# Chunked attention and a multiplicative FFN on one core: the first q and k as float32 through SyncE's queue, DMA transposes from group 12, another order of the first loads

## The chip, the cores and the metric

The kernel runs on one core of a Trainium2 chip. The core has five engines with queues of their own: TensorE (PE, matrix products and transposes), VectorE (DVE), ScalarE (ACT), GpSimd (POOL) and SyncE (SP). POOL and SP are used here to issue DMAs. The DMAs of both run on the same 16 DMA engines. The metric is the device time of one execution in microseconds (us). A time is the median of several runs; a profile is one execution, recorded by the hardware profiler.

## The reference

Eight batches of eight heads, 576 tokens and 64 columns per head go through softmax attention in chunks of 64 tokens; a chunk sees only itself. The heads are then put side by side (4608 tokens x 512 columns) and go through four weight matrices with one elementwise product:

```python
scores = scale * np.matmul(q_c, k_c.transpose(0, 1, 2, 4, 3))     # chunks of 64
scores = scores - np.max(scores, axis=-1, keepdims=True)
attn = np.exp(scores)
attn = attn / (np.sum(attn, axis=-1, keepdims=True) + 1e-09)
out = np.matmul(attn, v_c)
...
x = out.transpose(0, 2, 1, 3).reshape(B * S, H * D)               # 4608 x 512
a = x @ w1                                                        # 512 -> 1024
b = x @ w2
h = a * b @ w3                                                    # 1024 -> 1024
return (h @ w_out).astype(np.float32)                             # 1024 -> 512
```

All inputs and the output are float32 in DRAM.

## The kernel before

The kernel computes in bfloat16. Since no nonlinearity stands between w3 and w_out, it first multiplies the two once (w3o = w3 @ w_out, eight blocks of 128 rows, add_w3o) and then runs the FFN as (a * b) @ w3o.

The attention is cut into 36 groups of two chunks (128 tokens), all eight heads at once (add_group). For a group q and k are loaded (load_qk, line 220, two DMAs of 128 KB in bfloat16 through POOL's queue, which changes the type on the way; four half ones where a group crosses two batches, as group 4 does) into one of six "raw" buffers, tokens in the partitions. The products need the columns in the partitions, so q and k are transposed in one of two ways:

- on PE: eight transposes of 128 x 128 against an identity matrix (t_emit, line 274) into the one PSUM buffer p_tr, and then three copies by DVE or ACT: k to kT, and the two halves of q to a block-diagonal buffer qd (k_copy, q_copy);
- by DMA: one transposing DMA that SP issues (qk_turn, line 281) into kqT, from which k is used as it stands and q is copied to qd.

TURN_QK (line 23) says which group goes which way: 0 to 15 on PE, 16 to 35 by DMA. Then come the scores (s_emit, line 301, eight small matmuls into p_sc), maximum, difference, exponential, sum and normalisation on DVE and ACT, the transpose of the weights "an" (again on PE, at_emit with a copy, or by DMA, at_turn; TURN_A, line 24: by DMA from group 26), the product with v (av_emit, line 345) and the copy to xt.

The FFN goes over nine tiles of four groups (512 tokens, add_tile): for each of eight column blocks four matmuls with w1 and four with w2 (line 432), a copy and a product, and then four blocks of eight matmuls with w3o (line 457), a copy and an output write that SP issues.

No loop sets the order of all this. Every piece of work is an operation with a cost, a key and what it must wait for, and a planner (Plan.run, line 74) simulates the five engines ahead of time: each free engine takes the ready operation with the smallest key. POOL is the exception: it takes its operations, which are the loads and the making of the identity, in the order in which they are added, and that is the list LOADS (line 17), then the rest of the groups. A DMA occupies its engine's queue for its "issue", then moves along a ring; the planner lets two rings that are busy at once share the time in halves, and data count as landed after a further lag. At most eight DMAs are out on a ring. The order that comes out of the simulation is the order of each engine's program; on the chip an engine then keeps that order, and waits in it.

The PSUM is full: four "ffn" buffers, which the w3 blocks and the FFN share, and one each for p_sc, p_at, p_av and p_tr. At the beginning DVE clears the three qd and three vd buffers (lines 206 to 209).

Of the kernel before, what the change touches and what calls it, by code (L numbers as in the profile page):

```python
# [13 lines left out]

LOADS = [("wo", 0, 4), ("w3", 0, 1), ("ident",), ("qk", 0), ("qk", 1), ("wo", 4, 8), ("w3", 1, 2), ("qk", 2),
         ("w3", 2, 3), ("w3", 3, 4), ("qk", 3), ("w3", 4, 5), ("w3", 5, 6), ("qk", 4), ("qk", 5), ("w3", 6, 7),
         ("w12", 0, 2), ("v", 0), ("w3", 7, 8), ("qk", 6), ("qk", 7), ("w12", 2, 4), ("qk", 8), ("w12", 4, 6),
         ("v", 1), ("w12", 6, 8), ("qk", 9), ("qk", 10)]  # L20
TILES = [4] * 9

TURN_QK = [g >= 16 for g in range(36)]
TURN_A = [g >= 26 for g in range(36)]


class Op:
# [12 lines left out]
class Plan:  # L40
# [33 lines left out]
    def run(self):  # L74
        free = {e: 0.0 for e in ("PE", "ACT", "DVE", "POOL", "SP")}
        free["POOL"] = free["SP"] = 1.2
        todo = {e: [o for o in self.ops if e in o.engines] for e in free}

        rings, flown = {"POOL": [], "SP": []}, 0.0
        left, now, order, ends = len(self.ops), 0.0, [], [1.2]  # L80

        def heads(t):
            return [r[0] for r in rings.values() if r and r[0][0] <= t]

        while left or any(rings.values()):

            while flown < now:
                h = heads(flown)
                step = min([now - flown] + [x[1] * len(h) for x in h])
                step = min([step] + [r[0][0] - flown for r in rings.values() if r and r[0][0] > flown])  # L90
                flown = now if step >= now - flown else flown + step
                for x in h:
                    x[1] -= step / len(h)
                for r in rings.values():
                    if r and r[0] in h and r[0][1] < 1e-6:
                        o = r.pop(0)[2]
                        o.end = flown + o.lag
                        ends.append(o.end)
            for eng in free:
                if free[eng] > now or len(rings.get(eng, ())) >= self.RING:  # L100
                    continue
                if eng == "POOL":
                    pick = [o for o in todo[eng][:1] if self.ready(o, now)]
                else:
                    pick = [o for o in todo[eng] if self.ready(o, now)]
                if not pick:
                    continue
                o = min(pick, key=lambda o: o.key)
                for e in o.engines:
                    todo[e].remove(o)  # L110
                o.start, o.engine = now, eng
                cost = o.cost[o.engines.index(eng)] if isinstance(o.cost, tuple) else o.cost
                if o.issue:
                    free[eng] = now + o.issue
                    rings[eng].append([free[eng], cost, o])
                else:
                    free[eng] = now + cost
                    o.end = now + cost + o.lag
                    ends.append(o.end)
                for n in o.takes:  # L120
                    self.taken[n].append(o)
                order.append(o)
                ends.append(free[eng])
                left -= 1
            ends = [t for t in ends if t > now]
            h = heads(now)
            after = ends + [flown + x[1] * len(h) for x in h]
            assert after or not left, "the plan is stuck"
            now = max(min(after, default=now), now + 1e-6)
        return order  # L130
# [3 lines left out]
def kernel(  # L134
# [21 lines left out]
    C = 64  # L156
# [12 lines left out]
    bf = mybir.dt.bfloat16  # L169
    f32 = mybir.dt.float32  # L170

    BUFS = {"raw": 6, "kqT": 4, "kT": 3, "qd": 3, "vd": 3, "sd": 2, "e": 2, "an": 4, "at": 6, "w3t": 2, "abT": 2,
            "a_sb": 3, "o_sb": 4, "ffn": 4, "p_sc": 1, "p_at": 1, "p_av": 1, "p_tr": 1}

    consts = ctx.enter_context(tc.tile_pool(name="consts", bufs=1))
# [4 lines left out]
    def sb(tag, shape, dt=bf, bufs=None):  # L180
        return work.tile(shape, dt, tag=tag, name=tag, bufs=bufs or BUFS[tag])

    def ps(tag, shape, dt=f32):
        return psum.tile(shape, dt, tag=tag, name=tag, bufs=BUFS[tag])

    ident = consts.tile([P, P], bf)
    w1_sb = wpool.tile([P, KO, D_FF], bf, tag="w1")
    w2_sb = wpool.tile([P, KO, D_FF], bf, tag="w2")
    w3_sb = wpool.tile([P, FO, D_FF], bf, tag="w3")
# [22 lines left out]
    def load(cost, issue, emit, **kw):  # L212
        return plan.add("POOL", cost, 0, emit, lag=landing, issue=issue, **kw)
# [6 lines left out]
    def load_qk(g):  # L220
        (b0, c0), (b1, c1) = chunks(g)
        parts = [(slice(0, P), b0, c0, 2)] if b0 == b1 else [(halves[0], b0, c0, 1), (halves[1], b1, c1, 1)]
        box = raws[g] = {"ops": []}
        for w, src in enumerate((q, k)):
            for r, b, c, n in parts:
                def emit(eng, w=w, src=src, r=r, b=b, c=c, n=n):
                    if "t" not in box:
                        box["t"] = sb("raw", [P, 2, H, D])
                    nc.gpsimd.dma_start(box["t"][r, w], src[b, :, c * C:(c + n) * C, :].rearrange("h p d -> p h d"))  # L229
                box["ops"].append(load(0.43 * n, 0.5 + 0.2 * n, emit, takes=() if box["ops"] else ("raw",)))  # L230

    def load_v(b):
        v_got[b] = []
        for t in range(2):
            def emit(eng, t=t):
                nc.gpsimd.dma_start(vds[b % len(vds)][halves[t], :, :, t * D:(t + 1) * D].rearrange("p m c d -> p (m c) d"),  # L236
                                    v[b, NM * t:NM * (t + 1)].rearrange("h (c p) d -> p (h c) d", p=C))
            v_got[b].append(load(2.2, 1.17, emit, takes=() if t else ("vd",), after=(zero_v[b % len(vds)],)))

    def load_w12(j0, j1):  # L240
        for dst, w in ((w1_sb, moe_w1), (w2_sb, moe_w2)):
# [25 lines left out]
    def add_group(g, kt, ks, ka, kv):  # L267
# [6 lines left out]
        def t_emit(eng):  # L274
            t = box["tr"] = ps("p_tr", [P, 2, NM, P], bf)
            raw = raws[g]["t"]
            for w in (1, 0):
                for s in range(NM):
                    nc.tensor.transpose(t[:, w, s, :], raw[:, w, 2 * s:2 * s + 2, :].rearrange("p h d -> p (h d)"), ident[:])  # L279

        def qk_turn(eng):
            t = sb("kqT", [P, 2 * NM, P])
            nc.sync.dma_start_transpose(t[:], raws[g]["t"].rearrange("p w h d -> p (w h d)"))
            box["tr"] = t.rearrange("p (w s) t -> p w s t", w=2)
            box["kT"] = box["tr"][:, 1]
# [4 lines left out]

        def k_copy(eng):
            box["kT"] = sb("kT", [P, NM, P])
            copy(eng, box["kT"][:], box["tr"][:, 1, :, :])

        def q_copy(u):
            def emit(eng):
                copy(eng, qd[halves[u], :, :, u * C:(u + 1) * C].rearrange("p cc s t -> p s cc t"),
                     box["tr"][halves[u], 0, :, :].rearrange("p s (cc t) -> p s cc t", cc=2))
            return emit

        def s_emit(eng):
# [53 lines left out]

        got = raws[g]["ops"]
        if turned:
            tr = kc = plan.add("SP", 2.0, kt, qk_turn, after=got, takes=("kqT",), uses=[(got[0], "raw")], lag=2.5, issue=1.3)
            held, cost = [(tr, "kqT")], (0.35, 0.6)
        else:  # L360
            tr = plan.add("PE", 0.46, kt, t_emit, after=got + [made_ident], takes=("p_tr",), uses=[(got[0], "raw")], lag=0.2)
            held, cost = [(tr, "p_tr")], (0.43, 0.66)
            kc = plan.add(("DVE", "ACT"), cost, kt, k_copy, after=(tr,), takes=("kT",), uses=held)
# [7 lines left out]
        sm = plan.add("DVE", 1.1, ks, sum_emit, after=(ex,), lag=0.05)  # L371
        an = plan.add("DVE", 0.7, ks, norm_emit, after=(sm,), takes=("an",), uses=[(ex, "e")])
        if TURN_A[g]:
            ac = plan.add("SP", 1.0, ka, at_turn, after=(an,), takes=("at",), uses=[(an, "an")], lag=2.5, issue=1.3)
        else:
            at = plan.add("PE", 0.23, ka, at_emit, after=(an,), takes=("p_at",), uses=[(an, "an")], lag=0.2)
            ac = plan.add(("DVE", "ACT"), (0.43, 0.66), ka, at_copy, after=(at,), takes=("at",), uses=[(at, "p_at")])
# [99 lines left out]
    for what, *args in LOADS:  # L477
        if what == "ident":
            made_ident = plan.add("POOL", 0.6, 0, lambda eng: make_identity(nc, ident[:]), lag=0.3)
        else:  # L480
            {"qk": load_qk, "v": load_v, "w12": load_w12, "w3": load_w3, "wo": load_wo}[what](*args)
    landing = 2.5
# [5 lines left out]
            load_v(b)  # L488

    for g in range(NG):  # L490
        late = min(5 if g < 26 else 3, g // 2)
        add_group(g, *(3 * g - n + late for n in (30 if TURN_QK[g] else 28, 25, 19, 16)))
    for ko in range(FO):
        add_w3o(ko, 0.5 + ko)
# [2 lines left out]
        add_tile(g0, n, lambda j: 3 * g0 + 0.375 * n * j, lambda tk: 3 * (g0 + n) + 1 + 3 * tk)  # L497
        g0 += n
    for c, emit in sorted(outs, key=lambda x: x[0].key):
        plan.add("SP", 0.8, c.key, emit, after=(c,), uses=[(c, "o_sb")], lag=1.6, issue=0.4)  # L500

    with tc.manual_schedule():
        for o in plan.run():
# [31 lines left out]
```

## Time and profile before

| | |
|---|---|
| median of 3 runs | 257.01 us (256.85 to 257.58) |
| the profiled execution | 257.51 us, its span 255.7 us |
| PE busy (matmuls; weight loads) | 238.2 us, 93%; 125.9 us, 49% |
| DVE, ACT, POOL busy | 177.5 us (69%), 153.6 us (60%), 102.2 us (40%) |
| granted TensorE clock | 1.0 of full speed |
| DMA queue of POOL (software) | 118,688 packets, 19.41 MB |
| DMA queue of SP (hardware) | 31,888 packets, 16.00 MB |

The span is the time from the first to the last instruction that the profiler shows; the 1.8 us between it and the execution's time lie around it. "Busy" is the sum of an engine's instructions, and matmuls overlap, so a busy PE says little of how well it is used. The page's picture of the span in 40 slices of 6.4 us shows, for each, the busy tenths (9 is 90% or more) and the rate of the DMA engines:

```profile
PE   0469989899999999999999999999999999999994
...
DVE  7569999876989778788887877777768772222310
...
POOL 8856887989790964723392272000000000000000
...
GB/s 81 163 195 178 180 163 175 162 164 155 169 175 149 205 152 179 186 195 181 183 181 199 182 143 149 185 175 108 105 92 73 62 65 62 41 74 52 41 82 123
```

PE reaches nine tenths in the fourth slice. The DMA engines move 150 to 200 GB/s (bytes as written, so bfloat16 for the loads) from the second slice to the 27th, where the loads are through.

The DMAs by kind, with the median time from issue to landing:

```profile
raw<-in_q_dram POOLq DMA_DIRECT2D x32, 128.0 KB, 6.9
raw<-in_k_dram POOLq DMA_DIRECT2D x32, 128.0 KB, 6.7
...
kqT<-raw SPq DMA_TRANSPOSE x20, 7.0
...
at<-an SPq DMA_TRANSPOSE x10, 2.5
```

### The profile page before, as it was taken

Reading aid. Unit: us, or ns where it says so; the run is one execution under the profiler, and the core shown is the slowest. Engines: PE = TensorE matmul, PEld = TensorE weight load, DVE = VectorE, ACT = ScalarE, POOL = GpSimd, SP = SyncE. Lnnn points to the kernel's source line nnn. Section 1 sums busy time; section 2 is a strip of 40 time slices with the busy share of each in tenths; the row PEclk is TensorE's granted clock in tenths of the full one; section 3 lists DMA queues with packets and bytes.
Section 4 is the critical chain, followed back from the end, with each engine's and each line's share of the span. In section 5 each row is a group of like instructions: output and inputs, shape, how many; then the busy total and the mean of one; then the engine's idle time right before and its main releaser. Section 6 shows DMA issues by size and latency. Waiting matters only on the chain.

```text
span 255.7 us, 4814 instructions
## 1 busy us (share of the span) xinstructions
PE 238.2 (93%) x1808; PEld 125.9 (49%) x1808; DVE 177.5 (69%) x338; ACT 153.6 (60%) x268; POOL 102.2 (40%) x128
## 2 busy tenths in 40 slices
PE   0469989899999999999999999999999999999994
PEld 0345655456555555555555555444555444444443
DVE  7569999876989778788887877777768772222310
ACT  2247758668988776676766677756675443433232
POOL 8856887989790964723392272000000000000000
PEclk9999999999999999999999999999999999999999
DMA  5999999999999999999999999985422222111123
GB/s 81 163 195 178 180 163 175 162 164 155 169 175 149 205 152 179 186 195 181 183 181 199 182 143 149 185 175 108 105 92 73 62 65 62 41 74 52 41 82 123
DMA packets 150598, 35.70 MB, mean 140 GB/s; under 512 B 139696, under 2 KB 145072, under 8 KB 150576
## 3 DMA queue, kind: packets, MB, share of 16 engines
q0 software_dynamic: 118688, 19.41, 101.6%
q1 hardware_dynamic: 31888, 16.00, 28.7%
q8 instruction: 14, 0.23, 0.3%
q14 instruction: 8, 0.07, 0.1%
HBM read 38.80 MB, written 9.44 MB: 189 GB/s over the span
## 4 chain that ended last, share of the span: by engine, by line
PE 84%; DMA 8%; POOL 2%; ACT 2%; DVE 2%; issue 2%; ACTq 0%; POOLq 0%
PE ffn L432 48%; PE ffn L457 24%; DMA raw<-in_k_dram 5%; PE p_sc L307 3%; PE p_av L350 3%; DMA w_sb<-in_moe_w_dram 3%; PE p_tr L279 2%; PE p_at L339 2%; PE ffn L402 2%; ACT w3t L202 1%; POOL raw L229 1%; DVE qd L204 0%; POOL vd L236 0%; ACT kT L202 0%; DVE ss L327 0%
## 5 line engine op out<-in xcount | busy, mean ns | idle before, releaser
L432 PE MATMUL ffn<-xt,w_sb 128*128 128x512 bf16 x576 | 133.8, 379 | 0.0
L432 PEld LDWEIGHTS <-w_sb 128*128 128x128 bf16 x576 | 54.5, 98 | 60.9
L441 DVE TENSOR_TENSOR abT<-a_sb,ffn 128x512 bf16<-128x512 f32 x72 | 48.4, 673 | 33.1 <-PE ffn L432 31.5
L457 PE MATMUL ffn<-w3o_sb,abT 128*128 128x512 bf16 (+1 forms) x296 | 67.6, 374 | 0.0
L202 ACT COPY a_sb<-ffn 128x512 f32<-128x512 f32 x72 | 41.9, 582 | 27.2 <-PE ffn L432 26.8
L229 POOL DMA_DIRECT2D raw<-in_q_dram x40 | 34.5, 865 | 38.9 <-DMA kqT<-raw 32.4
L457 PEld LDWEIGHTS <-abT 128*128 128x128 bf16 x296 | 27.8, 98 | 29.2
L202 ACT COPY o_sb<-ffn 128x512 f32<-128x512 f32 (+1 forms) x32 | 18.3, 572 | 39.1 <-PE ffn L457 39.1
L327 DVE TENSOR_REDUCE ss<-e 128x8 f32<-128x512 bf16 x36 | 24.6, 682 | 17.3 <-ACT e L323 17.1
L229 POOL DMA_DIRECT2D raw<-in_k_dram x40 | 34.5, 869 | 4.4 <-DMA vd<-in_v_dram 3.1
L315 DVE TENSOR_REDUCE nm<-p_sc 128x8 f32<-128x512 f32 x36 | 24.5, 681 | 3.8 <-PE p_sc L307 3.7
L319 DVE TENSOR_TENSOR sd<-p_sc,nm 128x512 f32<-128x512 f32 x36 | 24.7, 685 | 0.4
L334 DVE TENSOR_TENSOR an<-e,rs 128x512 bf16<-128x512 bf16 x36 | 24.6, 684 | 0.0
L323 ACT ACTIVATE e<-sd 128x512 bf16<-128x512 f32 x36 | 22.7, 631 | 1.6 <-DVE sd L319 1.0
L202 ACT CAST xt<-p_av 128x512 bf16<-128x512 f32 x31 | 18.1, 585 | 8.6 <-PE p_av L350 8.4
L202 ACT COPY qd<-kqT 64x512 bf16<-64x512 bf16 x33 | 20.3, 616 | 0.3
L236 POOL DMA_DIRECT2D vd<-in_v_dram x16 | 18.6, 1176 | 1.9 <-DVE sd L319 1.1
L402 PE MATMUL ffn<-wo_sb,w3t 128*128 128x512 bf16 x64 | 16.7, 396 | 0.8 <-ACT w3t L202 0.7
L350 PEld LDWEIGHTS <-vd 128*128 128x128 bf16 x288 | 13.1, 98 | 8.3 <-issue 1.2
L307 PEld LDWEIGHTS <-qd 128*128 128x128 bf16 x288 | 12.3, 99 | 7.7 <-ACT qd L202 3.0
L350 PE MATMUL p_av<-at,vd 128*128 128x64 bf16 x288 | 14.3, 193 | 0.6 <-DVE xt L204 0.4
L202 ACT COPY qd<-p_tr 64x512 bf16<-64x512 bf16 x22 | 12.8, 580 | 2.0 <-DVE qd L204 1.6
(35 smaller groups left out, 154.4 us busy)
## 6 DMA issues: line engine op xcount, KB each, us to landing
out_dram<-o_sb SPq DMA_DIRECT2D x35, 256.0 KB, 2.3
vd<-in_v_dram POOLq DMA_DIRECT2D x16, 288.0 KB, 7.6
raw<-in_q_dram POOLq DMA_DIRECT2D x32, 128.0 KB, 6.9
raw<-in_k_dram POOLq DMA_DIRECT2D x32, 128.0 KB, 6.7
w_sb<-in_moe_w_dram POOLq DMA_DIRECT2D x8, 256.0 KB, 8.2
w_sb<-in_moe_w_dram POOLq DMA_DIRECT2D x16, 128.0 KB, 6.4
wo_sb<-in_moe_w_out_dram POOLq DMA_DIRECT2D x2, 512.0 KB, 7.3
raw<-in_q_dram POOLq DMA_DIRECT2D x8, 64.0 KB, 7.7
```

Source lines behind the costliest of these rows:

```text
L202: nc.scalar.copy(o, i)
L229: nc.gpsimd.dma_start(box["t"][r, w], src[b, :, c * C:(c + n) * C, :].rearrange("h p d -> p h d"))
L315: nc.vector.tensor_reduce(nm[:, :, 0], flat(box["sc"]), axis=AX.X, op=ALU.max)
L319: nc.vector.tensor_sub(sd[:], flat(box["sc"]), box["nm"].to_broadcast([P, 8, C]))
L323: nc.scalar.activation(e[:], box["sd"][:], ACT.Exp, scale=scale)
L327: nc.vector.reduce_sum(ss[:], box["e"][:], axis=AX.X)
L334: nc.vector.tensor_mul(an[:], box["e"][:], box["rs"].to_broadcast([P, 8, C]))
L350: nc.tensor.matmul(t[:, m, cc, :], vds[b % len(vds)][:, m, c, :], box["at"][:, 2 * cc + y, u * C:(u + 1) * C], start=True, stop=True)
L402: nc.tensor.matmul(box["wp"][:], box["t"][:, ki, :], wo_sb[:, ki, :], start=(ki == 0), stop=(ki == FO - 1))
L432: nc.tensor.matmul(t[:, :w], wt[:, ki, j * P:(j + 1) * P], x[:, ki, :], start=(ki == 0), stop=(ki == KO - 1))
L441: nc.vector.tensor_mul(box["abT"][:, j, :w], box["as", j][:, :w], box["b", j][:, :w])
L457: nc.tensor.matmul(t[:, :x1 - x0], box["abT"][:, ki, tk * P:(tk + 1) * P], w3o_sb[:, ki, x0:x1], start=(ki == 0), stop=(ki == FO - 1))
```

## The change

- WIDE = 3: q and k of groups 0, 1 and 2 are loaded as float32 into buffers "wide" of their own. SP issues these six DMAs (256 KB each), as the first that it does.
- They are transposed on PE as float32, against an identity in float32 (wide_ident, a copy of the other by DVE): q into an "ffn" buffer, k into p_tr, four transposes each (wide_emit). The copies to kT and qd change the type.
- TURN_QK begins at group 12 and TURN_A at group 24.
- LOADS has another order, without change in what POOL loads but for the three groups; the identity is made after seven loads, not after two.
- The planner: nothing moves on the rings before 3.4; the costs of v's loads, of the transposing DMAs and of the output writes are some 10% lower; the key that holds a group back ("late") goes by TURN_A.

```diff
+LOADS = [("wo", 0, 4), ("wo", 4, 8), ("w3", 0, 1), ("qk", 0), ("qk", 1), ("w3", 1, 2), ("w3", 2, 3), ("qk", 2),
+         ("qk", 3), ("ident",), ("w3", 3, 4), ("qk", 4), ("qk", 5), ("v", 0), ("w3", 4, 5), ("w3", 5, 6),
+         ("qk", 6), ("w12", 0, 2), ("w12", 2, 4), ("qk", 7), ("w12", 4, 6), ("w3", 6, 7), ("v", 1), ("qk", 8),
+         ("w3", 7, 8), ("qk", 9), ("w12", 6, 8), ("qk", 10)]
...
-TURN_QK = [g >= 16 for g in range(36)]
-TURN_A = [g >= 26 for g in range(36)]
+TURN_QK = [g >= 12 for g in range(36)]
+TURN_A = [g >= 24 for g in range(36)]
+LATE = 5
+
+WIDE = 3
...
-        rings, flown = {"POOL": [], "SP": []}, 0.0
+        rings, flown = {"POOL": [], "SP": []}, 3.4
...
+    wide_ident = consts.tile([P, P], f32)
...
-                        box["t"] = sb("raw", [P, 2, H, D])
-                    nc.gpsimd.dma_start(box["t"][r, w], src[b, :, c * C:(c + n) * C, :].rearrange("h p d -> p h d"))
-                box["ops"].append(load(0.43 * n, 0.5 + 0.2 * n, emit, takes=() if box["ops"] else ("raw",)))
+                        box["t"] = sb("wide", [P, 2, H, D], f32) if g < WIDE else sb("raw", [P, 2, H, D])
+                    queue = nc.sync if g < WIDE else nc.gpsimd
+                    queue.dma_start(box["t"][r, w], src[b, :, c * C:(c + n) * C, :].rearrange("h p d -> p h d"))
+                if g < WIDE:
+                    box["ops"].append(plan.add("SP", 0.43 * n, -1000 + g, emit, issue=0.6, lag=1.6,
+                                               takes=() if box["ops"] else ("wide",)))
+                else:
+                    box["ops"].append(load(0.43 * n, 0.5 + 0.2 * n, emit, takes=() if box["ops"] else ("raw",)))
...
-            v_got[b].append(load(2.2, 1.17, emit, takes=() if t else ("vd",), after=(zero_v[b % len(vds)],)))
+            v_got[b].append(load(2.0, 1.17, emit, takes=() if t else ("vd",), after=(zero_v[b % len(vds)],)))
...
+        def wide_emit(w):
+            def emit(eng):
+                t = box["tr", w] = ps("p_tr" if w else "ffn", [P, NM, P])
+                for s in range(NM):
+                    nc.tensor.transpose(t[:, s, :], raws[g]["t"][:, w, 2 * s:2 * s + 2, :].rearrange("p h d -> p (h d)"),
+                                        wide_ident[:])
+            return emit
...
-            tr = kc = plan.add("SP", 2.0, kt, qk_turn, after=got, takes=("kqT",), uses=[(got[0], "raw")], lag=2.5, issue=1.3)
+            tr = kc = plan.add("SP", 1.75, kt, qk_turn, after=got, takes=("kqT",), uses=[(got[0], "raw")], lag=2.5, issue=1.3)
             held, cost = [(tr, "kqT")], (0.35, 0.6)
+        elif g < WIDE:
+            trs = [plan.add("PE", 0.9, kt, wide_emit(w), after=got + [made_wide], takes=("p_tr" if w else "ffn",),
+                            uses=[(got[0], "wide")], lag=0.2) for w in range(2)]
+            tr, held, cost = trs[0], [(trs[0], "ffn")], (0.53, 0.59)
+            kc = plan.add(("DVE", "ACT"), cost, kt, k_copy, after=trs[1:], takes=("kT",), uses=[(trs[1], "p_tr")])
...
-            ac = plan.add("SP", 1.0, ka, at_turn, after=(an,), takes=("at",), uses=[(an, "an")], lag=2.5, issue=1.3)
+            ac = plan.add("SP", 0.88, ka, at_turn, after=(an,), takes=("at",), uses=[(an, "an")], lag=2.5, issue=1.3)
...
+            made_wide = plan.add("DVE", 0.2, -2000, lambda eng: nc.vector.tensor_copy(wide_ident[:], ident[:]), after=(made_ident,))
...
-        late = min(5 if g < 26 else 3, g // 2)
+        late = min(LATE if not TURN_A[g] else 3, g // 2)
...
-        plan.add("SP", 0.8, c.key, emit, after=(c,), uses=[(c, "o_sb")], lag=1.6, issue=0.4)
+        plan.add("SP", 0.7, c.key, emit, after=(c,), uses=[(c, "o_sb")], lag=1.6, issue=0.4)
```

## The prediction

> **What bounds the kernel now.** I read first what TensorE (PE) waited for (columns: total us, times, longest), since PE is busy for 93% of the span:
>
> ```profile
> PE ffn L391 <- DMA w_sb<-in_moe_w_dram: 8.9, 1, 8.9
> PE p_sc L307 <- ACT qd L202: 1.8, 1, 1.8
> PE p_tr L279 <- DMA raw<-in_k_dram: 1.6, 3, 0.8
> ...
> ```
>
> One wait of 8.9 us stands at the very start, for the first block of w3; all others are under 2 us. The table of stages says where the rest went:
>
> ```profile
> 0.00:8.87 8.87, 0.00 (x0) 0.00 (x0) 6.55 (x6) 1.28 (x1) 7.75 (x15) 1.00 0.80 102
> 8.87:24.00 15.13, 11.79 (x115) 7.79 (x116) 10.19 (x21) 8.81 (x14) 9.85 (x15) 1.00 1.68 185
> 24.00:48.00 24.00, 22.06 (x226) 13.27 (x225) 22.49 (x48) 16.02 (x28) 19.17 (x26) 1.00 1.92 172
> 48.00:252.40 204.40, 204.32 (x1471) 104.81 (x1469) 138.24 (x267) 127.16 (x227) 65.40 (x75) 1.00 1.25 134
> ```
>
> (Stage, its length, busy us of PE, weight loads, VectorE (DVE), ScalarE (ACT) and GpSimd (POOL); clock, DMA share, GB/s.) From 48 us on PE is idle for 0.08 us in 204: there only less PE work shortens the run. Before 48 it is idle for 8.87 + 3.34 + 1.94 = 14.15 us: there the order in which data arrive decides. The chain of waits gives the full-rate price of each block (start, length):
>
> ```profile
> 10.68 1.03 PE p_tr L279 x8
> ...
> 83.05 0.45 PE p_tr L279 x8
> ...
> 100.87 0.23 PE p_sc L307 x8
> 101.10 1.73 PE ffn L457 x8
> 102.83 3.46 PE ffn L432 x16
> 106.28 0.23 PE p_av L350 x8
> ```
>
> So a matmul of 512 columns costs 0.216, a group's eight transposes 0.45 (1.03 early on), scores and values 0.23 each; four p_at transposes take half of eight, 0.225. Times the counts (576 + 288 + 64 of 512 columns, 16 transposed groups, 26 p_at, 36 + 36 small blocks, 64 w3 transposes) PE has 234.0 us of work; its last matmul ends at about 252.4, so 18.4 us are lost, nearly all before 48. I use that sum below.
>
> **The change, part by part.**
>
> *Groups 12 to 15 turned by DMA, weights of 24 and 25 too.* This takes 4 x 0.45 + 2 x 0.225 = **2.25 us off PE**, all of it in the full stretch, so it counts whole. Their copies for kT and at (0.41 to 0.59 us) leave DVE and ACT too. In return SyncE's (SP's) queue issues four transposes of 1.24 us and two of 1.2, with the output writes in line behind them. A kqT lands in 7.0 us (median of 20). Cover: group 12's scores ran at 72.6, and its FFN tile, the fourth, starts at about 42.5 + 3 x 4 x 5.87 = 113 (5.87 us per group is the chain's period), 40 us later. Groups 16 to 35 go this way already and PE has 0.08 us idle. So delay costs nothing; with the cover gone, the price is in the rivals. The altered planner costs and LATE only move keys in this full stretch: nothing either, between -0.1 and +0.1.
>
> *The six loads that go to SP.* They take 6 x 0.89 = 5.3 us off POOL's issuing and raw buffers off three groups; POOL did not bind, so 0 for that. What counts is when they land, and this hangs on how 16 DMA engines serve two queues. The trace shows such sharing at 100 us, where a kqT (256 B packets) meets loads (128 B packets):
>
> ```profile
> 99.00:100.00 1.00, 1.00 (x6) 0.45 (x5) 0.97 (x4) 0.70 (x2) 0.00 (x0) 1.00 2.39 152
> 100.50:102.50 2.00, 2.00 (x26) 1.17 (x22) 1.97 (x4) 1.69 (x3) 2.00 (x3) 1.00 1.60 159
> 90.40:90.90 0.50, 0.50 (x4) 0.20 (x2) 0.47 (x2) 0.00 (x0) 0.50 (x2) 1.00 1.30 281
> ```
>
> Loads alone move 152 GB/s, so 1,190 packets per us; the transpose almost alone 281 GB/s (1,055 per us in the packet records). Together 159 GB/s is 414 pairs of 128 + 256 B, and the records count 405 and 418 per us: **one packet for one packet**, whatever they weigh. A load of q or k to SP is 1,024 packets of 256 B (128 rows x 8 heads), six are 6,144. The weights they meet are w_out in 1,024 packets of 1,024 B (170 per us when alone, 3.9 to 5.5 us) and w3 in 128 packets of 2,048 B a block (about 101 per us from 207 GB/s at 12 to 14 us). One for one, SP's small packets get only the rate of the big ones.
>
> [...]
>
> Step by step. POOL's first packet flew at 3.2. SP's can come between 2.2 and 3.2 (the first output write: issue 67.48, packet 69.59; SP can issue from about 0.9); I take 2.7, and 0.5 us x 1,055 = 530 packets ahead. w_out: 1,024 pairs at 5.9 ns (SP's hidden) to 6.8 ns (added up), taken 6.4: until 9.7, SP at 1,554. Three w3 blocks: 384 pairs at 10.3 ns: until 13.7, SP at 1,938. q and k of group 3 are 2,048 small packets: 408 pairs per us (row above) to 607 (half of 1,214); I take 550, as both are plain copies: until 17.4, SP at 3,986. The fourth w3 block: until 18.7, 4,114. The last 2,030 beside group 4 at 550: until **22.4**. Landing adds 1.3 (w3's first packets were through at about 7.55, PE started at 8.87). So group 1 is there at 20.0 and group 2 at 23.7, where before PE transposed them at 13.8 and 18.1.
>
> *PE's order.* SP's and w_out's planned costs are equal (6 x 0.86 and 8 x 0.64, each about 5.1) and the planner halves time between queues from 3.4: group 2 is planned ready at 13.7 + 1.6 = 15.3, w3's first block at 15.0 + 1.6 = 16.6. So PE's program has the float32 transposes of groups 0, 1 and 2 ahead of all w3 work. If group 2 is late, w3 blocks that landed from 12 us on wait behind it.
>
> *The float32 transposes.* No row shows one. From below: 0.45 a group, as bf16. From above: the planner's 2 x 0.9 at the early rate (1.03 for 0.45), 4.1. I take 1.8; only group 2's is on the path, those before lie in the wait for data. [...]
>
> *The identity.* POOL makes it after seven loads, at about 1.25 + 0.88 + 0.8 + 3 x 0.55 + 2 x 0.9 + 0.6 = 7.0. The float32 copy on DVE (0.2) is planned for 7.65, behind a memset:
>
> ```profile
> 7.73 1.98 DVE L208 MEMSET vd<- 128x2304 uint32 x1 [0.43 <-issue]
> ```
>
> so it is there at about 9.9, and q, k copies behind it wait no longer than their data. Group 0 lands after that (2,048 packets: about 15.2), so 0; if data came early it is the gate. The copies out of float32 PSUM cost DVE up to 0.69 for 0.42 (the o_sb copy against qd): at most 0.8 us per group, in DVE's idle time of that stretch (4.9 of 15.1).
>
> **Sum.** Group 2's transposes end at 23.7 + 1.8 = 25.5. By then PE has done three transposed groups, two scores, two p_at: 1.35 + 0.46 + 0.45 = 2.26 of full-rate work. Left: 234.0 - 2.25 - 2.26 = 229.5. After that PE has four w3 blocks in stock (2.2 each) and values sooner (v ahead of six w3 and w12 loads), so of the 2 us idle after 24 I keep 1.0. End: 25.5 + 229.5 + 1.0 = 256.0, where it was 252.4: **+3.6 us**. The profiled execution (257.51, span 255.7) would be 261.1; the median of the runs lies 0.5 lower, 257.0: forecast **260.6**. Ends: earliest SP packets, everything hidden and a 0.45 block give group 2 at 21.6 and 257.2; no head start, pairs added up at 408 and a block of 4.1 give group 2 at 27 and 266; 4.1 and no overlap at once are unlikely, so 265.
>
> **Rivals.**
> A, above: 260.6, its own range 257.2 to 265.
> B, faster: the queues share the time, not the packets. Then six loads of 0.86 us at half rate from 2.2 or 3.2 are through at about 12, landed at 13.3; PE starts when the identity is there, 10.0, and is through with group 2 at 10 + two slow blocks + one = 17.5. End 17.5 + 229.5 + 2 = 249.0, -3.4: 253.6. For it: the planner assumes it. Against: 405 to 418 per us above. It decides if group 2 lands before about 20.
> C, faster: the start stays as good as now, because w3 work stands ahead of group 2 or fills the wait; only the 2.25 us remain: 254.8. For it: lost time was 18.4 already. Against: planned 15.3 against 16.6.
> D, slower: the four new kqT slow the loads. Each holds them at 405 instead of 1,190 per us for 2.5 us, 1.7 us lost, four times 6.7 us. If PE's stock of 40 us were gone, -2.25 + 6.7 = +4.5: 261.5 on an unchanged start.
>
> **Chances.** A 0.55, B 0.22, C 0.13, D 0.06, 0.04 for nothing gained (0.02 the same, 0.02 slower). About 0.3% (0.8 us) is what a measurement here can tell from no change. A's lower end gives 0.03 to the same, C 0.03. Faster: 0.22 + 0.10 = 0.32; same: 0.03 + 0.03 + 0.02 = 0.08; slower: 0.52 + 0.06 + 0.02 = 0.60. The range runs from B, 253.4, to 265.
>
> **What would show it.** A: PE idle between 12 and 24 us for k of groups 1 and 2 (wide), with w3's first block landed long before its transposes; p_tr of group 2 after 21 us. B: group 2 transposed by 18 us, L391 begun by 18. C: L391 ahead of group 2's transposes. From 48 us on no new idle time, and L279 down to nine groups; a wait there for kqT speaks for D. The forecast is wrong above all if the wide loads land in the order and time that the planner has.

## The result and the profile after

| | before | after |
|---|---|---|
| median | 257.14 us (256.85 to 257.58, 4 runs) | 264.81 us (262.91 to 266.56, 4 runs) |
| ratio | | 1.0295, 95% interval 1.0221 to 1.037 |
| profiled execution, its span | 257.51, 255.7 us | 266.56, 264.8 us |

The changed kernel is slower by 7.7 us. Its profiled execution is the longest of its four runs, 9.05 us above the profiled one of before. Ratios, here and below, leave out a run that is over 1.5% above the fastest of its kernel (263.96 us in e9, 267.81 in e12), while medians have every run.

In the profile of after, the lines of the program have moved: load_qk is L234, the bfloat16 transposes L288, the float32 ones L294, the transposes and product of w3 L413 and L424, the FFN L454 and L479. What PE waited for (total us, times, longest):

```profile
PE ffn L294 <- DVE wide_ident L502: 9.8, 1, 9.8
PE ffn L294 <- DMA wide<-in_q_dram: 5.2, 2, 4.0
PE p_tr L294 <- DMA wide<-in_k_dram: 3.0, 2, 1.5
...
PE p_av L367 <- ACT qd L206: 1.2, 1, 1.2
```

The picture of the span in 40 slices (6.6 us each) has PE at nine tenths from the fifth slice on, that is from about 26.5 us; before, nine tenths came in the fourth slice, of 6.4 us each:

```profile
PE   0314999999999999999999999999998999999995
```

The one long wait at the start is now for the float32 identity, and 8.2 us of waits for SP's loads stand behind it. The same stages as before (columns as there):

```profile
0.00:8.87 8.87, 0.00 (x0) 0.00 (x0) 6.55 (x6) 1.28 (x1) 6.27 (x14) 1.00 0.86 141
8.87:24.00 15.13, 5.88 (x35) 4.62 (x36) 6.69 (x13) 2.27 (x4) 6.14 (x8) 1.00 1.37 182
24.00:48.00 24.00, 21.93 (x216) 14.82 (x218) 18.08 (x38) 15.98 (x27) 18.58 (x26) 1.00 1.79 171
48.00:252.40 204.40, 201.74 (x1441) 103.53 (x1467) 146.16 (x285) 126.58 (x222) 66.02 (x76) 1.00 1.40 139
```

From 8.87 to 24 us PE has 35 matmuls where it had 115, and DVE falls from 10.19 to 6.69 us busy, ACT from 8.81 to 2.27: the chain of the groups nearly stands still. The 2.66 us idle of the last row are too many, since some matmul records are missing there (556 of 576 in one FFN line); the weight loads are complete (x576), and I use them below.

The timeline of PE shows the float32 transposes (start, length, then in brackets the idle time ahead and its cause):

```profile
9.84 1.11 PE L294 MATMUL ffn<-wide_ident,wide 128*128 128x128 f32 x4 [9.84 <-DVE wide_ident L502]
10.75 1.06 PE L294 MATMUL p_tr<-wide_ident,wide 128*128 128x128 f32 x4
...
17.19 1.12 PE L294 MATMUL ffn<-wide_ident,wide 128*128 128x128 f32 x4 [4.01 <-DMA wide<-in_q_dram]
19.80 1.09 PE L294 MATMUL p_tr<-wide_ident,wide 128*128 128x128 f32 x4 [1.50 <-DMA wide<-in_k_dram]
...
23.47 1.11 PE L294 MATMUL ffn<-wide_ident,wide 128*128 128x128 f32 x4 [1.21 <-DMA wide<-in_q_dram]
26.06 1.09 PE L294 MATMUL p_tr<-wide_ident,wide 128*128 128x128 f32 x4 [1.48 <-DMA wide<-in_k_dram]
26.94 1.06 PE L413 MATMUL ffn<-ident,w_sb 128*128 128x128 bf16 x8
```

Group 1 is transposed at 17.2 and 19.8, group 2 at 23.5 and 26.1, where PE had them at 13.7 and 18.1 before. The first w3 block had landed at 14.4 and is transposed only at 26.94, behind group 2 in PE's program. The timeline of SP's queue shows the six loads being issued:

```profile
0.74 0.46 SPq L234 DMA_DIRECT2D wide<-in_q_dram  x1
...
2.79 2.56 SPq L234 DMA_DIRECT2D wide<-in_k_dram  x1
5.40 8.30 SPq L234 DMA_DIRECT2D wide<-in_q_dram  x1
13.74 3.53 SPq L234 DMA_DIRECT2D wide<-in_k_dram  x1
```

An issue takes 0.46 us at first and 8.30 for the fifth load. When that one began, at 5.40, four loads (4,096 packets) had been issued and about 2,040 packets were through; when it ended, at 13.70, 3,072 were. So it was held while some 2,000 packets stood in line and drained slowly. The DMAs by kind (median us from issue to landing):

```profile
raw<-in_q_dram POOLq DMA_DIRECT2D x29, 128.0 KB, 10.6
```

A load of q on POOL's queue now takes 10.6 us where it took 6.9.

**Turns.** Counted from the packet records of the trace, packets that start in each stretch on POOL's and on SP's queue:

| us | POOL moves | POOL | SP (256 B) |
|---|---|---|---|
| 2.5 to 3.5 | nothing yet | 0 | 1,040 |
| 5 to 6 | w_out, 1,024 B | 142 | 65 |
| 9 to 10 | w_out, 1,024 B | 146 | 148 |
| 10 to 11 | w_out, 1,024 B | 151 | 153 |
| 13 to 14 | w3, 2,048 B | 90 | 96 |
| 14 to 15 | w3, 2,048 B | 87 | 93 |
| 17.5 to 18.5 | q, k, 128 B, and 2 of w3 | 608 | 290 |
| 23 to 24 | q, k, 128 B | 403 | 419 |
| 26 to 27 | q, k, 128 B | 1,206 | 0 (through) |

With every kind of neighbour there are stretches of one packet for one packet: 9 to 17 us, 18.5 to 20 and 22 to 24. There the two queues alternate closely: over the 600 packets from 9 to 11 us, SP's count less POOL's stays within a band of 8, where the same packets in random order would spread over about 30. Between these stretches SP got less: under half of POOL's number from 5 to 6 and from 17.5 to 18.5 us, though it had packets issued; why is not shown.

SP's 1,024th packet is through at 3.2 us, and each further 1,024th at 5.6, 13.7, 18.3, 21.9 and 25.4. The loads themselves landed at 4.0, 9.6, 17.1, 19.7, 23.4 and 25.9: the second load landed well after the 2,048th packet, so the packets do not go strictly load by load.

**Where PE's time went.** I price every weight load that PE has issued by then at the full rate (0.216 us with a matmul of 512 columns, 0.0565 with 128, 0.0288 with 64) and subtract the sum from the elapsed time. A float32 transpose is priced like a bfloat16 one, so what it takes more counts as lost. What is left is lost time:

| by us | 12 | 18 | 24 | 27 | 36 | 48 | 56 to 185 | 200 on |
|---|---|---|---|---|---|---|---|---|
| before | 10.5 | 14.0 | 14.9 | 15.1 | 15.7 | 18.1 | 18.1 | 18.1 |
| after | 11.6 | 17.1 | 22.4 | 25.1 | 27.4 | 28.1 | 28.2 | 29.6 |

So 10.1 us more are lost by 56 us, 1.4 more near 198, and the work itself is 2.3 us less (235.5 to 233.2 by these prices): together +9.2, against the 9.05 between the two profiled executions. The scores of groups 1 to 5 reach ACT's exponentials at 27.7, 33.4, 38.4, 42.8 and 47.1, before at 19.3, 24.3, 28.9, 33.1 and 37.7; the first FFN matmul starts at 48.1 instead of 42.5.

The stall near 198, by the timelines of SP's queue and of PE:

```profile
188.57 0.53 SPq L488 DMA_DIRECT2D out_dram<-o_sb  x1
196.68 1.23 SPq L300 DMA_TRANSPOSE kqT<-raw  x1
```

```profile
200.55 0.41 PE L367 MATMUL p_av<-at,vd 128*128 128x64 bf16 x8 [1.19 <-ACT qd L206]
```

The last group's transpose by DMA is issued only at 196.68; the copy of its q on ACT waits 3.4 us for it, and PE waits for ACT. It could not be issued sooner: the last load of k was issued at 173.6 us and landed only at 196.5, before at 153.9 and 165.6.

### The profile page after: what moved, and what is told of

The parts are those of the page before. It is cut to its first block, busy times and chain, and to the rows that moved or that the text cites. A ratio compares the mean times of both kernels' runs of the same rounds, so it can differ in the third digit from the quotient of the medians.

```text
span 264.8 us, 4718 instructions
## 1 busy us (share of the span) xinstructions
PE 238.7 (90%) x1736; PEld 127.8 (48%) x1768; DVE 178.2 (67%) x340; ACT 149.8 (57%) x261; POOL 97.0 (37%) x122
## 4 chain that ended last, share of the span: by engine, by line
PE 86%; DMA 6%; SPq 5%; ACT 1%; issue 1%; DVE 0%; ACTq 0%
PE ffn L454 46%; PE ffn L479 23%; PE ffn L424 5%; SPq L234 5%; DMA wide<-in_k_dram 5%; PE p_av L367 3%; PE p_sc L324 3%; PE p_at L356 2%; PE ffn L413 2%; PE p_tr L288 1%; DMA kqT<-raw 1%; PE p_tr L294 0%; ACT w3t L206 0%; DVE xt L208 0%; ACT qd L206 0%
## 5 line engine op out<-in xcount | busy, mean ns | idle before, releaser
L454 PE MATMUL ffn<-xt,w_sb 128*128 128x512 bf16 x556 | 132.8, 379 | 1.0
L454 PEld LDWEIGHTS <-w_sb 128*128 128x128 bf16 x576 | 54.0, 98 | 59.3
L479 PE MATMUL ffn<-w3o_sb,abT 128*128 128x512 bf16 (+1 forms) x289 | 67.0, 373 | 0.4
L234 POOL DMA_DIRECT2D raw<-in_q_dram x37 | 31.6, 859 | 41.6 <-DMA kqT<-raw 17.0
L479 PEld LDWEIGHTS <-abT 128*128 128x128 bf16 x296 | 28.0, 98 | 29.7 <-issue 0.2
L234 POOL DMA_DIRECT2D raw<-in_k_dram x37 | 31.6, 856 | 23.4 <-DMA vd<-in_v_dram 11.8
L206 ACT COPY o_sb<-ffn 128x512 f32<-128x512 f32 (+1 forms) x33 | 18.9, 573 | 34.3 <-PE ffn L479 33.4
L344 DVE TENSOR_REDUCE ss<-e 128x8 f32<-128x512 bf16 x36 | 24.5, 681 | 13.7 <-ACT e L340 13.6
L206 ACT COPY qd<-kqT 64x512 bf16<-64x512 bf16 x39 | 24.0, 615 | 7.8 <-DMA kqT<-raw 7.4
L332 DVE TENSOR_REDUCE nm<-p_sc 128x8 f32<-128x512 f32 x36 | 24.3, 675 | 2.5 <-PE p_sc L324 2.5
L294 PE MATMUL ffn<-wide_ident,wide 128*128 128x128 f32 x12 | 3.3, 434 | 15.1 <-DVE wide_ident L502 9.8
L324 PEld LDWEIGHTS <-qd 128*128 128x128 bf16 x288 | 12.9, 101 | 7.7 <-issue 1.6
L424 PE MATMUL ffn<-wo_sb,w3t 128*128 128x512 bf16 x59 | 16.1, 392 | 0.4 <-issue 0.2
## 6 DMA issues: line engine op xcount, KB each, us to landing
raw<-in_q_dram POOLq DMA_DIRECT2D x29, 128.0 KB, 10.6
```

Of the source, the lines that this page charges most:

```text
L206: nc.scalar.copy(o, i)
L234: queue.dma_start(box["t"][r, w], src[b, :, c * C:(c + n) * C, :].rearrange("h p d -> p h d"))
L332: nc.vector.tensor_reduce(nm[:, :, 0], flat(box["sc"]), axis=AX.X, op=ALU.max)
L344: nc.vector.reduce_sum(ss[:], box["e"][:], axis=AX.X)
L424: nc.tensor.matmul(box["wp"][:], box["t"][:, ki, :], wo_sb[:, ki, :], start=(ki == 0), stop=(ki == FO - 1))
L454: nc.tensor.matmul(t[:, :w], wt[:, ki, j * P:(j + 1) * P], x[:, ki, :], start=(ki == 0), stop=(ki == KO - 1))
```

## The experiments

All times are medians, each ratio is against the kernel before on the same chip (its medians there: 257.43, 257.12 and 257.26). "Lost" is the measure of the table above; e1 to e12 are the runs by the numbers in their names.

**Parts alone.** First the change with no group in float32, so that only the list of loads, the planner's numbers and the turns are left:

```diff
-WIDE = 3
+WIDE = 0
```

> The changed kernel with WIDE = 0: groups 0 to 2 come in bfloat16 through POOL again, in the place that the new list gives them; all else of the change stays. Theory P (SP's small packets get one turn for each big packet of POOL, and PE's program waits for them): the waits for the wide loads go; PE starts at about 12.5 to 14 us, with w3's first block or group 0, since w_out is first in the list, and then runs through: 255.5 to 258.5 us. Rival O (w_out ahead of all is what costs): 262 to 265. Rival T (the six more DMA transposes cost): 261 to 264.

e1 took 260.74 us, 1.0133 [1.0098, 1.0168], lost 23.3, between what was expected of the theory and of its rivals. The waits of PE tell why this is not a clean reading:

```profile
PE p_tr L288 <- POOL ident masks.py:199: 15.5, 1, 15.5
```

With q and k of groups 0 to 2 on POOL's queue again, the identity stands behind more loads there, and POOL makes it only at 15.5 us. So the same was run with the identity after three loads:

```diff
-LOADS = [("wo", 0, 4), ("wo", 4, 8), ("w3", 0, 1), ("qk", 0), ("qk", 1), ("w3", 1, 2), ("w3", 2, 3), ("qk", 2),
-         ("qk", 3), ("ident",), ("w3", 3, 4), ...
+LOADS = [("wo", 0, 4), ("wo", 4, 8), ("w3", 0, 1), ("ident",), ("qk", 0), ("qk", 1), ("w3", 1, 2), ...
```

> As e1_no_wide (no float32 loads; the new list, the moved transposes), with the identity after three loads instead of after the loads of group 3: in e1 PE began at 15.5 us, when the identity came, so the list and the identity's place were not told apart. If the identity was e1's cost: PE begins at 11.5 to 13 us with w3's first block, 256 to 258.5 us. If the list with w_out in front costs by itself: 259.5 to 261, as e1.

e9 took 258.97 us, 1.0073 [1.0044, 1.0101], lost 21.7, between the two expectations. PE's first wait is now for the first w3 block, which lies behind both halves of w_out:

```profile
PE ffn L413 <- DMA w_sb<-in_moe_w_dram: 12.0, 1, 12.0
```

The identity's place was worth 1.8 us to the run ahead. Next the turns alone, on the kernel before:

```diff
-TURN_QK = [g >= 16 for g in range(36)]
-TURN_A = [g >= 26 for g in range(36)]
+TURN_QK = [g >= 12 for g in range(36)]
+TURN_A = [g >= 24 for g in range(36)]
...
-        late = min(5 if g < 26 else 3, g // 2)
+        late = min(5 if not TURN_A[g] else 3, g // 2)
```

> The kernel before with only the transposes moved: q and k by DMA from group 12, weights from 24 (late goes by TURN_A). P: 2.25 us off PE and nothing else, 254.3 to 255.5 us, and no new idle time of PE after 48 us. T: the four further kqT hold the loads up, 257 to 260.

e2 took 256.77 us (10 runs), 0.9972 [0.9942, 1.0003]: 0.7 us for 2.25 of work taken off PE, and not told apart from nothing; neither expectation was met. Lost time is 17.8 until 185 us; then it rises by 1.3 until 215. The last load of k is issued at 164.7 us and lands at 190.2, before at 153.9 and 165.6. So the loads do run later with more transposes beside them, and in this trace it is at their end that this is felt, not in the middle.

And the turns taken back in the changed kernel:

```diff
-TURN_QK = [g >= 12 for g in range(36)]
-TURN_A = [g >= 24 for g in range(36)]
+TURN_QK = [g >= 16 for g in range(36)]
+TURN_A = [g >= 26 for g in range(36)]
```

> The changed kernel with the DMA transposes from 16 and 26 again. P: PE has 2.25 us more to do and the stall near 198 us (1.4 us in the profile) goes: 265 to 267.5. T (moved transposes cost): 261 to 263.5.

e11 took 267.5 us, 1.0396 [1.0366, 1.0426], so the turns give 2.7 us here by the medians. Its lost time is flat at 27.4 to the end, with no stall near 198. Over all kernels, with one trace of each, a rise by over 1 us after 100 us came in four of the ten with the turns (after, e2, and e12 and e6 below) and in none of the four with 16 and 26. The three rises near 200 us (after, e2, e12) are in the three traces where the last load of k landed latest: at 190.2 us in e2 and at 196.5 to 196.6 in the others, against 187.7 or sooner in the eleven other traces. That fits the wait for the last transpose, but it is a pattern of single traces, not a test. The rise of e6 lies between 120 and 185 us and is not explained.

**PE's order.** The planner is told when the wide loads really land, and has the groups' transposes in turn, so that PE's program no longer has them ahead of all w3 work:

```diff
+LAND = (1.6, 1.6, 8.6, 9.5, 11.5, 12.4)
...
-    plan = Plan(BUFS, ("qd", "kT", "kqT", "sd", "e", "an", "at"))
+    plan = Plan(BUFS, ("qd", "p_tr", "kT", "kqT", "sd", "e", "an", "at"))
...
-issue=0.6, lag=1.6,
+issue=0.6, lag=LAND[2 * g + w],
```

> The changed kernel, with the planner told when the six wide loads were seen to land (lags of 1.6, 1.6, 8.6, 9.5, 11.5, 12.4 in place of 1.6; p_tr is taken in the order of the groups). The DMAs and their order stay; PE's program now has w3 work ahead of groups 1 and 2. P: the loads land as late as before, but w3's first blocks, which landed from 14.4 us on, are used: 5 to 6.5 us come back, 258.3 to 260 us. Rival (the data, not the order of PE's program, bound the start): 263 to 266.

e3 took 265.35 us, 1.0334 [1.0264, 1.0404], as its rival had it. PE did fill its waits: lost time is 21.0 at 30 us, where the changed kernel has 26.2. But it is 26.1 at 48 and 28.6 at 65. In its waits a new one has come:

```profile
PE p_at L357 <- DVE an L352: 4.8, 3, 4.1
```

The exponentials of groups 1 and 2 came at 27.1 and 34.6, no sooner than the 27.7 and 33.4 of the changed kernel. The work that PE did early here only moved its idle time to where it waits for the groups. That the arrival of the groups' data decides is argued from this, not shown by this run alone: with w3 ahead, group 2's float32 transposes began at 28.5, though its data had landed at 26.1, so the new order also held the groups back a little.

**The queue.** The wide loads on POOL's queue instead of SP's:

```diff
-                    queue = nc.sync if g < WIDE else nc.gpsimd
-                    queue.dma_start(box["t"][r, w], src[b, :, c * C:(c + n) * C, :].rearrange("h p d -> p h d"))
...
+                    nc.gpsimd.dma_start(box["t"][r, w], src[b, :, c * C:(c + n) * C, :].rearrange("h p d -> p h d"))
```

> The changed kernel, with the six float32 loads issued by POOL at their places in the list; float32 transposes, identity and copies stay. P: one queue, so no turns to share, PE starts with w3's first block at about 12.5: 256.5 to 259.5 us. Rival F (the float32 transposes, copies and identity cost the time): 262 to 266.

e4 took 263.6 us, 1.0243 [1.0209, 1.0277], lost 26.5. PE waits 16.3 us for the identity here, behind POOL's loads as in e1, so this does not price the queue. Against e1 it says something of the float32 form: the two have the same list and one queue, and the three groups as float32 instead of bfloat16 cost 2.9 us (263.6 against 260.74), 0.8 of it in the wait for the identity.

The wide loads with the list of before:

```diff
-LOADS = [("wo", 0, 4), ("wo", 4, 8), ("w3", 0, 1), ("qk", 0), ("qk", 1), ...
+LOADS = [("wo", 0, 4), ("w3", 0, 1), ("ident",), ("qk", 0), ("qk", 1), ("wo", 4, 8), ...
```

> The changed kernel with the old list of loads, so with the identity after two loads again; three groups still come as float32 through SP. P, as it stands after the first runs (SP's packets get one turn for each big packet of POOL; groups 1 and 2 come late; from there the chain of the groups through DVE, some 4.5 us each, is late, and with it the FFN): the weights at POOL's head are as big, SP's 6,144 packets last until 24 to 27 us, 262 to 267 us. Rival O (the new list is what costs): 256 to 258.

e5 took 268.83 us, 1.0469 [1.0391, 1.0546], above what was expected. The waits of PE:

```profile
...
PE ffn L294 <- DMA wide<-in_q_dram: 6.7, 1, 6.7
PE p_tr L294 <- DMA wide<-in_k_dram: 6.2, 2, 3.8
```

Here a block of w3, in packets of 2,048 B, flies between the two halves of w_out, and SP's 3,072nd packet is through at 16.0 us, its last at 28.0, where after had 13.7 and 25.4. Part of this is no matter of turns one for one: from 5 to 7 us SP moved 29 packets beside 314 of POOL's, with about 2,000 issued and not yet moved. Against the turns alone (256.77) the wide loads, with their float32 form and the planner's numbers, cost 12.1 us with this list; with the list of the change they cost 264.81 - 258.97 = 5.8, the identity's place included.

**The size of the other queue's packets.** If turns go by packets, smaller packets on POOL's queue must give SP more. w_out was loaded in quarters of its columns, 256 B a packet, and the identity made first:

```diff
+LOADS = [("ident",), ("wo", 0, 4), ...
...
-            nc.gpsimd.dma_start(wo_sb[:, k0:k1, :], ...)
+            for c in range(0, D_MODEL, P):
+                nc.gpsimd.dma_start(wo_sb[:, k0:k1, c:c + P], ...[:, k0:k1, c:c + P])
```

> The changed kernel with w_out loaded in column quarters, packets of 256 B in place of 1,024 B (eight DMAs for two), and the identity first in the list. P (turns by packet): SP gets four turns where it had one, its 6,144 packets are through at 13 to 18 us instead of 25.4, group 2 is transposed before 20 us instead of 26; w3's first block lands later; 258 to 262 us. Rival (queues share by time or by bytes): SP's packets through at 24 us or later as before, 263 to 267.

e8 took 259.59 us, 1.0095 [1.0061, 1.013], as expected. SP's 1,024th packet and each further one are through at 3.2, 4.4, 6.7, 9.3, 12.8 and 19.4 us, the last later than expected. From 10 to 14 us both queues move some 340 packets per us (1,330 and 1,385 in all), where beside 1,024 B it was 150. Ahead of that the shares jump: SP 666 against 183 from 5 to 6 us, and 57 against 660 from 9 to 10; why is not shown. The issue of the fifth load in SP's queue, and PE's float32 transposes of groups 1 and 2:

```profile
3.67 2.32 SPq L234 DMA_DIRECT2D wide<-in_q_dram  x1
```

```profile
10.78 1.09 PE L295 MATMUL ffn<-wide_ident,wide 128*128 128x128 f32 x4
...
14.39 1.10 PE L295 MATMUL ffn<-wide_ident,wide 128*128 128x128 f32 x4
...
20.02 1.09 PE L295 MATMUL p_tr<-wide_ident,wide 128*128 128x128 f32 x4 [4.53 <-DMA wide<-in_k_dram]
```

The issue of 8.30 us has become 2.32, and group 1 no longer waits for its loads. The exponentials of groups 1 to 5 come at 21.6, 27.4, 32.4, 36.8 and 41.1, each 6.0 to 6.1 us earlier than in the changed kernel, the first FFN matmul at 42.1 instead of 48.1, and lost time at 48 us is 22.0 instead of 28.1: the delay of the first groups goes through the chain unchanged to the FFN. To see what the identity had of this, it alone was moved:

```diff
+LOADS = [("ident",), ("wo", 0, 4), ...
```

> The changed kernel with the identity first in the list, as in e8_small_wo, but w_out in its whole rows. P: group 0 is transposed at 4 to 7 us instead of 9.8, groups 1 and 2 as late as before (17 and 26): 263.5 to 266, so e8's 5.2 us came from the size of the packets. Rival (the identity's place made e8's gain): 258.5 to 261.

e12 took 265.04 us, 1.0278 [1.0206, 1.035], with four runs from 263.14 to 267.81 (263.47 without the longest): not told apart from the change. The fifth load's issue in SP's queue and PE's transposes of group 2's k:

```profile
3.76 7.97 SPq L234 DMA_DIRECT2D wide<-in_q_dram  x1
```

```profile
25.53 1.09 PE L294 MATMUL p_tr<-wide_ident,wide 128*128 128x128 f32 x4 [2.87 <-DMA wide<-in_k_dram]
```

Group 0 is transposed at 4.2 us instead of 9.8, and group 2 still at 25.5; the late rise is there again. The lost time at 185 us, ahead of that rise, tells the parts: 28.2 in the changed kernel, 27.4 in e12 and 22.1 in e8. So 0.8 us are the identity's place and 5.3 are w_out in 256 B packets. That e8 also loads w_out by eight DMAs instead of two was not separated from the size.

**Only one group wide.** SP had some 2,000 packets through by 5 us, which is as many as group 0 has. With the list of before, one group in float32, first with the turns of the change:

```diff
-WIDE = 3
+WIDE = 1
```

> As e5_old_list, but WIDE = 1: only group 0 through SP. P: its 2,048 packets fit into the 2 us in which SP's queue is alone (2,019 had passed at 5 us in the changed kernel); group 0 is transposed at 7 to 8.5 us instead of 10.7, POOL's next groups come 1.7 us sooner, the chain of the groups starts some 3 us sooner: 252.5 to 255 us. Rival O: as e5, 256 to 258. Rival F (float32 itself costs): not under 257.

e6 took 260.34 us, 1.0123 [1.0064, 1.0182], above what was expected. The start is better, lost time 13.1 at 24 us (14.9 before); but 18.9 at 65, and after rises between 120 and 185 it is 21.9. With the turns at 16 and 26:

> As e6_wide_one, with the DMA transposes from 16 and 26 as before. P: PE has 2.25 us more work, but the loads are not held up by the six further DMA transposes: 253.5 to 256 us; against e6 it shows again what the moved transposes are worth (e2 gave 0.7 of the 2.25).

e7 took 258.51 us, 1.005 [1.0033, 1.0067], again above. Here the moved transposes cost: with them, in e6, it is 1.8 us more. Lost time is 13.2 at 24 us, 18.0 at 48 and 19.0 after 65: the 2 us are given back before the FFN is under way, which begins at 42.9; the first v had landed at 33.9 and 35.8. To see whether that late v is the cause, v and the first FFN weights were loaded earlier:

```diff
-         ("w3", 2, 3), ("w3", 3, 4), ("qk", 3), ("w3", 4, 5), ("w3", 5, 6), ("qk", 4), ("qk", 5), ("w3", 6, 7),
-         ("w12", 0, 2), ("v", 0), ("w3", 7, 8), ...
+         ("w3", 2, 3), ("w3", 3, 4), ("qk", 3), ("w3", 4, 5), ("qk", 4), ("v", 0), ("w3", 5, 6), ("w12", 0, 2),
+         ("qk", 5), ("w3", 6, 7), ...
```

> As e7_wide_one_16_26 (group 0 alone through SP, old list, old transposes), with v of the first batch and the first block of w1 and w2 some 6 us earlier in the list. In e7 PE had lost 13.2 us at 24 us (before: 14.9), but 18.0 at 48 (before: 18.05), as the FFN began at 42.9 behind v's landing. If the start's gain was given back for want of v: the FFN begins at 34 to 37, 253.5 to 256 us. Rival (group 0 sooner is worth nothing, the groups' chain through DVE or the loads behind set the FFN's pace): 257.5 to 259.5.

e10 took 257.39 us (10 runs), 0.9997 [0.9978, 1.0015]. The first FFN matmul moved to 34.8 as expected, and the time did not: lost time is 13.6 at 24 us, 17.2 at 48 and 17.9 in the end, as before. No version was shown to be faster than the kernel before.

## Why the prediction was right, and where its sizes were off

The direction and the mechanism (rival A) were right; the size was not: +7.7 us against a forecast of +3.6. That 264.81 lies 0.2 us inside the upper end of the range, 265, is luck: that end stood for no head start and a float32 block of 4.1 us, and neither came about. Step by step:

- **One packet for one packet: shown, with exceptions.** The records count it in most of the time from 9 to 24 us, in close alternation (148 and 146 packets from 9 to 10 us, 96 and 90 from 13 to 14, a band of 8 over 600 packets), and smaller packets on the other queue brought SP's loads sooner and saved 5.3 us of lost time (e8 against e12). The exceptions are stretches such as 5 to 7 us in e5 (29 against 314) and 9 to 10 us in e8 (57 against 660), where SP got far less. Alone, SP moved 1,040 packets of 256 B in 1 us (2.5 to 3.5 us), and POOL 287 of w_out's 1,024 B in the 1.6 us from 3.9 to 5.5 in the kernel before. At these rates the 148 and 146 packets are, by my estimate, 0.14 and 0.81 us of work: equal numbers were no equal shares of the time, which speaks against rival B.
- **Head start and rates: both mis-sized, in opposite directions.** SP flew from 1.87 and POOL's first packet came at 3.89 (2.98 before; the 3.2 that I had read is not in the trace), so SP was 1,740 packets ahead, not 530. But w_out was through at 12.6 us and not at 9.7, three w3 blocks at 16.9 and not at 13.7, and beside q and k the queues made some 400 pairs per us at best (403 and 419 from 23 to 24) and not the 550 that I took. So at 18.7 us SP was at 4,253 packets, close to the forecast 4,114, and group 1's k was there at 19.7, close to the forecast 20.0, because two errors cancelled. The last 1,890 packets, beside the fourth w3 block and groups 3 and 4, then took 6.7 us where I had 3.7: SP was through at 25.4 instead of 22.4. From there PE began 0.65 us later and not 1.3 (the 7.55 behind my 1.3 is misread too: w3's first block was through at 8.56), and only k's half of the float32 block was left. The transposes of group 2 ended at 26.9 instead of 25.5, and PE had done a little less by then: lost time 25.1 instead of the sum's 23.2, **1.9 us**.
- **Float32 block: right.** Four take 0.91 (9.84 to 10.75) and 0.88 us (26.06 to 26.94), so 1.8 for a group as taken; the eight bfloat16 transposes of w3 behind them took 0.85. The 0.45 at the lower end of A's range, the price of a bfloat16 block, is not seen: a float32 transpose costs 0.22 us here (0.88 / 4), twice a bfloat16 one at that time (0.85 / 8, so 0.11). Only 0.9 of the 1.8 lay on the path, as q's half was done while k was still on its way.
- **Identity: right in time** (9.84 against 9.9). But group 0 landed at 9.6 and not at 15.2, so the identity was the gate for group 0, the case that the prediction named for early data. It is worth 0.8 us (e12).
- **"I keep 1.0" of idle after group 2: mis-sized by 2.1 us.** 3.1 were lost from 27 to 56 us. I had PE's stock of w3 work fill the wait. But the groups come one per 4 to 6 us, by the exponentials, and from group 1 on they were 8 to 10 us late; the FFN waits for four of them. In e3 the work in stock filled nothing for good, and e8 shows that the delay goes through whole. The same holds for "PE's order": the in-order wait was there, but taking it away gained nothing.
- **The turns: 2.25 us off PE, shown in the work** (2.3). In time they gave 2.7 us in the changed kernel (e11), 0.7 on the kernel before (e2, not told apart from nothing), and cost 1.8 with one group wide (e6 against e7). "So delay costs nothing" failed for one place: **1.4 us** near 198, in the profiled execution. Rival D had the mechanism, later loads, but neither their end as the place nor the size. The rise came in four of ten kernels with the turns, three times where the last load of k landed latest; what decides whether it comes is open. Also open is whether it stands in the median: the median of after lies 1.75 us below its profiled run, and no other run of it has a trace.
- "From 48 us on no new idle" was wrong by that stall; the float32 waits between 12 and 24 us and group 2 after 21 us were as forecast.

The three terms make 1.9 + 2.1 + 1.4 = 5.4 of the 5.5 us by which the profiled execution exceeded the sum. Within the 7.7, the list of loads with the planner's numbers has 2.2 (258.97 against 256.77), which I had not priced by itself. The float32 form cost up to 2.9 on one queue (e4 against e1); the price of SP's queue with the identity in the same place was not separated from it. Why a better start (e7, e10) is given back between 24 and 65 us was not settled; later loads are argued, not shown.

## What to carry to other kernels

Before moving loads to an idle queue, compare packet sizes: in these traces a queue of 256 B packets beside one of 1,024 or 2,048 B ones got one packet for each of them (148 against 146 and 96 against 90 in 1 us of after), and at times less (65 against 142). Count what its head start can carry: here some 2,000 packets, one group of the three, though moving just that group gained nothing either (1.005 in e7). And follow early data to the next stage's own gate: a start with 1.7 us less lost by 24 us (13.2 in e7 against 14.9) was worth nothing by 48 us (18.0 against 18.1), and with the values and the first weights sooner the time was that of before (0.9997, e10).

## What was unexpected of the hardware

- Issuing on SP's queue is not a fixed cost: 0.46 us for the first load, 8.30 and 10.13 for the fifth when about 2,000 packets were in line (after, e5), 2.32 when they drained faster (e8: 3,072 packets through at 6.7 us, against 13.7 and 16.0).
- POOL's first packet came 0.91 us later (3.89 against 2.98) when SP's packets flew from 1.87. It is so in every trace: 3.75 to 4.02 us in the nine with early packets on SP's queue, 2.84 to 2.98 in the five without; why is not shown.
- The runs of after spread from 262.91 to 266.56, those of before from 256.85 to 257.58.
